# Row tables of the decays turned out of stage 0's table, and a prologue in a new order

## The chip, the cores and the metric

The kernel runs on one core of a Trainium2 chip. The metric is the device time of one launch, in microseconds. The five engines named below are TensorE (PE, with its weight loads as PEld), VectorE (DVE), ScalarE (ACT), GpSimd (POOL) and SyncE (SP, which only issues DMAs here). Each engine runs its own list of instructions in order, and waits on semaphores where it needs another engine or a DMA.

## The reference: what is computed

A linear attention with a decaying state (4 batches, 8 heads, 768 tokens, head size 48) is followed by a two-layer network. For each batch and head, over tokens t:

```
y[t]  = r[t] @ (state + outer(u * k[t], v[t]))
state = w[:, None] * state + outer(k[t], v[t])
x     = y with heads joined: (3072 tokens, 384)
h     = x @ w_in;  out = max(0.01 * h, h) @ w_out      # 384 -> 2048 -> 384
```

## The kernel before

The 768 tokens of a batch are cut into 6 chunks of 128. A **stage** n is one chunk of one batch, 24 in all: stages 0 to 3 are the first chunks of the four batches, 4 to 7 the second ones, and so on. Inside a chunk the recurrence is done by matrix products: r is scaled by w to the power (t - 64), k by w to the power (63 - t), so that the product of the two holds the decay between two tokens. The scale factors stand in **row tables** `qtab` and `ktab` (128 tokens x 384 head columns), which every stage except stage 0's first use multiplies into its r and k.

The work of one stage, with the names that the order list uses:

- `k3 r3 v3`: loads of 128 x 384 blocks in f32, cast to bf16 by the DMA (line 224, issued by POOL; stage 0's k and r come uncast over ACT's and SP's queues, line 215). `wi0` to `wi3` and `wo0` to `wo3` are quarters of the two weight matrices (lines 234 and 238, also POOL).
- `P3q`, `P3k`: DVE multiplies r by `qtab` and k by `ktab` (line 373).
- `T3q`, `t3q`: PE turns the product (four matmuls with the identity, line 436), ACT copies it out of PSUM (line 454; `t5q@` means that DVE does it). From stage 6 on a DMA transpose does both (`X6T`, line 378, issued by SP).
- `A3`: the 128 x 128 products of the turned pairs (PE, line 465). `M3a`, `M3b`: DVE masks them (lines 474 and 478).
- `X3 D3 Q3` (stages below 4) or `q4 Q4` (stages 4 and up): the diagonal term with u. `q4` is three DVE operations (lines 402, 404, 406) into `s_tok`; `Q4` is two POOL operations of 128 x 512 (line 413).
- `K3`, `S3`: the chunk's share of the state (PE, line 506) and its decay (DVE, lines 569, 572, 574).
- `Y3`, `y3`: the stage's output (PE, lines 597 and 604), copied by ACT into `xT` (line 618).
- `G3.1`, `g3.1`: a quarter of the first layer for one stage (12 matmuls, line 643; ACT, line 653). `J2.6`, `j2.6`: an eighth of it for the pair of stages 4 and 5 (6 matmuls of 256 columns, line 666; ACT, line 676).
- `H1`, `h1`: the second layer for one stage (16 matmuls, line 690; ACT, line 702; SP sends it out, line 704). It needs all of `w_out_sb`.
- `F6`: six matmuls on ones (line 271), whose result nobody reads. They wait only for the PSUM bank that comes next.

Two things set the order of the work. The **prologue**, up to stages 6 and 7, is the list `ORDER`, written out by hand: each name adds its instructions to its engine's list, so the list's order is the order on each engine, POOL's and SP's queues included. PSUM's eight banks are handed out in the same order, each from the bank that was given back longest ago. After it a loop over pairs of stages runs (lines 747 to 786): first layer of one pair, second layer of the pair before, attention of the pair after.

The tables before the change: `w` is loaded once as rows of one partition (line 709) and once by head (line 712). The by-head copy is turned by `Cw` (line 525), `Wl` takes its logarithm (line 544), and `E` makes `turned` (line 337): for each pair of heads the powers of w, with head columns on partitions and tokens along the row, q's half and k's half. `turned` scales stage 0's r and k after they were turned, so stage 0 doesn't wait for the row tables (`t0q`, `t0k`, line 449). The row copy goes another way: `bc` spreads it over 128 partitions by one-partition f32 matmuls (line 318), `lnw` takes its logarithm (line 325), and two exponentials with a scale for each token make `qtab` and `ktab` (line 332; `exps` makes the second scale, line 289).

Of the kernel before, what the change touches and what calls it, by code (L numbers as in the profile page):

```python
# [27 lines left out]
w8 k0 r0 w u8 u one trow ones tcol wlz r1 table tri id8 zr v0y k1 F6 Cw Wl exps id wi1 E v0z c0k@ k3 qk0 F11 T0k bc r3  # L28
c0q@ W wu8 t0k u16 T0q v0 lnw Cu t0q U qtab r2 C utab F2 A0 X0 P1q ktab v1 D0 M0a T1q wi3 P1k t1q P0k F6 T1k k2 P3k M0b
t1k F5 T3k v3 P3q F1 A1 t3k X1 Q0 r4 F1 D1 M1b T3q K0 k4 Y0 P2q t3q M1a K1 y0 A3 r5 Q1 T2q S1 G0.1 t2q k5 M3a Y1 g0.1  # L30
X3 wi2 G0.3 M3b y1 wi0 P2k G1.3 g0.3 S0 v2 D3 T2k g1.3 Q3 G1.1 t2k P4q v5 K3 P4k Y3 g1.1 X2 wo1 T4q P5q y3 D2 S3 T4k
t4q T5q v4 q5 G3.1 t4k A2 r6 t5q A4 g3.1 G3.3 wo3 P5k G1.2 M2a g3.3 Q5 M2b G3.2 g1.2 q4 G0.2 g3.2 G0.0 g0.2 k6 K2 g0.0
T5k Q2 G1.0 Q4 S2 t5k Y2 g1.0 A5 y2 G3.0 M5b k7 G2.3 M5a g3.0 M4a G2.2 wo2 g2.3 M4b K4 Y5 wo0 g2.2 S4 Y4 y5 r7 G2.1 P6q
y4 k8 J2.1 g2.1 J2.6 r8 q6 j2.1 J2.5 j2.6 r9 J2.3 j2.5 k9 P7k J2.4 j2.3 P6k J2.7 X6T Q6 j2.4 J2.2 j2.7 G2.0 j2.2 J2.0
g2.0 k10 H1 P7q j2.0 v11 q7 X7T v6 v7 P8k H0 h1 P8q Q7 q8 X8T P9q v8 H3 h0 v10 P9k q9 X9T r11 r10 A6 h3 A7 M6a H2 v9
M7a k11 M7b M6b Q9 K6 Y6 h2 S6 Y7 y6 K7 y7 Q8 K5 S7 S5
# [7 lines left out]
class Sched:  # L44
# [7 lines left out]

    def add(self, eng, emit, R=(), W=(), dma=None):
        o = Op()
        o.eng, o.emit, o.dma, o.inc, o.val = eng, emit, dma, False, None
        deps = []
        for key in R:
            w = self.writer.get(key)
            if w is not None:
                deps.append((w, True))  # L60
        for key in W:
            w = self.writer.get(key)
            if w is not None:
                deps.append((w, False))
            for r in self.readers.get(key, ()):
                deps.append((r, False))
        o.deps = []
        for d, raw in deps:
            if d.dma is None and d.eng == eng and dma is None and (eng == "pe" or not raw):
                continue  # L70
            if d is not o and d not in o.deps:
                o.deps.append(d)
        for key in R:
            self.readers.setdefault(key, []).append(o)
        for key in W:
# [51 lines left out]
def bass_rwkv5_eagle__then__act_leaky_relu_kernel(  # L127
# [13 lines left out]
    def SB(name, shape, dt=BF16):  # L141
        return ctx.enter_context(nc.sbuf_tensor(name, shape, dt))
# [7 lines left out]
    w_row = SB("w_row", [128, HD // 2], FP32)  # L150
    u_row = SB("u_row", [1, HD], FP32)
    one_row = SB("one_row", [128, 128], FP32)
# [7 lines left out]
    lnw = SB("lnw", [128, HD], FP32)  # L160
# [9 lines left out]
    kexp = SB("kexp", [128, 1], FP32)  # L170
# [137 lines left out]
    w_bank = []  # L308

    def spread_w():  # L310
        for half in range(2):
            w_bank.append(take())
        assert w_bank[1][1][1] == w_bank[0][1][1] + 1

        def emit():
            for half in range(2):
                at0 = slice(64 * half, 64 * half + 1)
                last = PE.matmul(w_bank[half][0][:, 0:192], one_row[at0, :], w_row[at0, :], start=True, stop=True)
            return last

        add("pe", emit, R=["one_row", "w_row"], W=[w_bank[0][1], w_bank[1][1]])

    def log_w():
        i = w_bank[0][1][1]
        add("act", lambda: A.activation(lnw[:, :].rearrange("p (two c) -> p two c", two=2),
                                        ps_all[:, i:i + 2, 0:192], AF.Ln),
            R=[w_bank[0][1], w_bank[1][1]], W=["lnw"])
        give(w_bank[0][1])
        give(w_bank[1][1])
# [366 lines left out]
    def g2_out(n, c0=0, c1=HD):  # L696
# [147 lines left out]
```

## Time and profile before

| what | before |
|---|---|
| time, median of 3 runs | 169.48 us (169.34 to 171.7) |
| the profiled execution's own time | 169.59 us |
| its span, first to last instruction | 167.8 us |
| PE busy | 162.7 us of the span |
| DVE, ACT, POOL busy | 110.5, 91.3, 110.8 us |
| fillings in the prologue (matmuls on ones) | 32 |
| first second-layer matmul in the chain | 38.02 us |

All times inside a profile are counted from the span's first instruction. A line of the timeline has the start in us, the time from there to the end of the last of the merged instructions, the engine, the line, the operation, and in brackets how long the engine had been idle and what ended that. Instructions of one engine overlap a little: the next one starts some 0.1 us before the one before has ended, so on a busy engine the distance between two starts counts. A line of the chain has start, length, and what the time is put down to. A second-layer block for one stage is 16 matmuls in 2.60 us, a `G` block 0.67 us, a `J` block 0.66 us.

### The profile page before, as it was taken

What the parts mean: (1) busy time and instruction counts of PE and PEld (TensorE: products, weight loads), DVE (VectorE), ACT (ScalarE), POOL (GpSimd) and SP (SyncE); (2) the same over time, 40 slices, a digit from 0 to 9 for tenths busy, and PEclk for the clock granted to TensorE, in tenths of its full rate; (3) what the DMA queues carried; (4) which work ended last, traced back from release to release, by engine and by line L of the source; (5) the groups of instructions that cost most, each with busy time, mean ns of one, the idle gap of its engine ahead of it and who ended that gap; (6) DMA issues with size and microseconds to landing.
All of it is one profiled execution on the core that took longest, in us unless ns stands there. A gap on an engine that the chain in (4) does not pass through costs nothing.

```text
span 167.8 us, 4861 instructions
## 1 busy us (share of the span) xinstructions
PE 162.7 (97%) x2089; PEld 123.1 (73%) x2089; DVE 110.5 (66%) x224; ACT 91.3 (54%) x168; POOL 110.8 (66%) x125
## 2 busy tenths in 40 slices
PE   5999999999999999999999999999999999999994
PEld 4577899996668768668668768678678678668563
DVE  7889696928885597596599998996996805000000
ACT  6944888893127437438437537537437447449221
POOL 8999969999997839939949976966960540000000
DMA  7999999999999995996994997995996111011012
GB/s 109 137 158 153 191 178 157 128 170 147 173 148 200 144 127 154 90 101 172 97 131 139 122 141 147 145 126 117 149 98 152 24 47 51 0 47 51 30 63 96
DMA packets 101267, 20.18 MB, mean 120 GB/s; under 512 B 94459, under 2 KB 101246, under 8 KB 101246
## 3 DMA queue, kind: packets, MB, share of 16 engines
q0 software_dynamic: 76512, 10.03, 95.5%
q1 hardware_dynamic: 23694, 9.65, 30.4%
q8 instruction: 16, 0.26, 0.6%
q10 hardware_dynamic: 1040, 0.20, 0.6%
q14 instruction: 5, 0.04, 0.1%
HBM read 20.45 MB, written 4.72 MB: 150 GB/s over the span
## 4 chain that ended last, share of the span: by engine, by line
PE 90%; POOL 4%; DMA 4%; ACT 1%; issue 0%; POOLq 0%
PE ps L690 38%; PE ps L666 32%; PE ps L643 7%; PE ps L604 6%; DMA v_sb<-in_v_dram 4%; PE ps L465 4%; PE ps L506 2%; POOL r_sb L224 2%; PE ps L436 1%; POOL k_sb L224 1%; ACT xT L618 1%; POOL v_sb L224 1%; POOL w_in_sb L234 0%; PE ps L597 0%; POOL trow L256 0%
## 5 line engine op out<-in xcount | busy, mean ns | idle before, releaser
L690 PE MATMUL ps<-w_out_sb,gT 128*128 128x384 bf16 (+2 forms) x400 | 65.6, 320 | 0.0
L413 POOL TENSOR_TENSOR at<-ident,s_tok 128x512 bf16<-128x512 bf16 x40 | 42.5, 1099 | 20.4 <-DVE s_tok L406 20.4
L666 PE MATMUL ps<-xT,w_in_sb 128*128 128x256 bf16 x480 | 55.1, 273 | 0.2 <-ACT xT L618 0.2
L690 PEld LDWEIGHTS ps<-w_out_sb,gT 128*128 128x128 bf16 x400 | 37.7, 98 | 22.4
L676 ACT ACTIVATE gT<-ps 128x512 bf16<-128x512 f32 x80 | 47.8, 597 | 9.2 <-PE ps L666 4.5
L666 PEld LDWEIGHTS ps<-xT,w_in_sb 128*128 128x128 bf16 x480 | 46.4, 98 | 6.9 <-ACT xT L618 0.3
L702 ACT ACTIVATE out_sb<-ps 128x384 f32<-128x384 f32 (+2 forms) x25 | 11.9, 478 | 55.6 <-PE ps L690 55.6
L478 DVE CAST_PREDICATED at<-mask,ps 128x512 bf16<-128x512 uint16 x40 | 24.8, 685 | 21.5 <-PE ps L465 21.5
L224 POOL DMA_DIRECT2D k_sb<-in_k_dram x23 | 21.5, 934 | 4.2 <-PE ps L666 4.2
L224 POOL DMA_DIRECT2D v_sb<-in_v_dram x24 | 22.0, 922 | 0.0
L224 POOL DMA_DIRECT2D r_sb<-in_r_dram x23 | 21.1, 923 | 0.1
L404 DVE TENSOR_TENSOR rku<-r_sb,ku 128x384 bf16<-128x384 bf16 x20 | 17.1, 856 | 0.7
L643 PE MATMUL ps<-xT,w_in_sb 128*128 128x128 bf16 x192 | 12.8, 224 | 0.0
L373 DVE TENSOR_TENSOR qk<-r_sb,qtab 128x384 bf16<-128x384 bf16 x23 | 10.2, 444 | 3.9 <-DMA r_sb<-in_r_dram 3.9
L574 DVE TENSOR_TENSOR st<-sum_t,wl 128x384 bf16<-128x384 bf16 x16 | 11.7, 730 | 0.5
L643 PEld LDWEIGHTS ps<-xT,w_in_sb 128*128 128x128 bf16 x192 | 11.5, 101 | 0.5
L406 DVE TENSOR_REDUCE s_tok<-rku 128x8 f32<-128x384 bf16 x20 | 11.1, 553 | 0.7
L618 ACT ACTIVATE xT<-ps 128x384 bf16<-128x384 f32 x24 | 10.8, 490 | 1.0 <-PE ps L604 0.8
L653 ACT ACTIVATE gT<-ps 128x512 bf16<-128x512 f32 x16 | 9.6, 599 | 2.7 <-PE ps L643 2.1
L604 PE MATMUL ps<-at,v_sb 128*32 128x128 bf16 x384 | 10.9, 223 | 0.0
L373 DVE TENSOR_TENSOR qk<-k_sb,ktab 128x384 bf16<-128x384 bf16 x23 | 8.8, 387 | 0.8 <-DMA k_sb<-in_k_dram 0.8
L604 PEld LDWEIGHTS ps<-tp,st 128*32 128x32 bf16 x240 | 7.2, 96 | 2.7 <-issue 2.5
(66 smaller groups left out, 122.5 us busy)
## 6 DMA issues: line engine op xcount, KB each, us to landing
out_dram<-out_sb SPq DMA_DIRECT2D x23, 192.0 KB, 2.2
v_sb<-in_v_dram POOLq DMA_DIRECT2D x24, 96.0 KB, 6.5
r_sb<-in_r_dram POOLq DMA_DIRECT2D x23, 96.0 KB, 5.9
k_sb<-in_k_dram POOLq DMA_DIRECT2D x23, 96.0 KB, 6.1
w_in_sb<-in_moe_w_in_dram POOLq DMA_DIRECT2D x4, 384.0 KB, 7.8
w_out_sb<-in_moe_w_out_dram POOLq DMA_DIRECT2D x4, 384.0 KB, 8.3
tp<-qk SPq DMA_TRANSPOSE x18, 5.1
k_f<-in_k_dram ACTq DMA_DIRECT2D x1, 192.0 KB, 2.7
```

The costliest lines, as they stand in the source:

```text
L224: add("pool", lambda: G.dma_start(dst, src), R=pace, W=[(which, n)], dma=f"{which}{n}")
L373: add("dve", lambda: V.tensor_tensor(qk[iq][:, H * half:H * half + H, 0:D], hd(src), hd(tab[:, :]), ALU.mult), R=[(name, n), "qk"[half] + ...
L404: add("dve", lambda: V.tensor_tensor(rku[i2][:, :], r_of(n), ku[i2][:, :], ALU.mult), R=[("r", n), ("ku", i2)], W=[("rku", i2)])
L413: add("pool", lambda hh=hh, s_of=s_of: G.tensor_tensor(at[ia][:, hh, :, :], ident[:, :].unsqueeze(1).to_broadcast([128, NP, 128]), s_of.un ...
L478: add("dve", lambda: V.copy_predicated(at[n % NAT][:, hh, :, :], mask[:, :].bitcast(mybir.dt.uint16).unsqueeze(1).to_broadcast([128, NP, 1 ...
L604: last = PE.matmul(ps_y[32 * q:32 * q + 32, 128 * s:128 * s + 128], a, m, start=not whole and step == 0, stop=step == len(columns[q]) - 1)
L618: add("act", lambda: A.activation(xT[m % NX][:, :, 128 * half:128 * half + 128], ps_y[:, 0:HD].rearrange("p (s t) -> p s t", t=128), AF.Copy),
L643: last = PE.matmul(ps_g[:, 128 * f:128 * f + 128], w_in_sb[:, s, 128 * fb:128 * fb + 128], xT[ix][:, s, t], start=s == 0, stop=s == NSL - 1)
L666: last = PE.matmul(ps_g[:, 256 * f:256 * f + 256], w_in_sb[:, s, 128 * fb:128 * fb + 128], xT[ix][:, s, :], start=s == 0, stop=s == NSL - 1)
L676: add("act", lambda: A.activation(gT[ig][:, 2 * j:2 * j + 2, :].rearrange("p f t -> p (f t)"), ps_g[:, :], AF.Prelu, alpha=0.01), R=[key], ...
L690: last = PE.matmul(ps_o[:, 0:c1 - c0], gT[ig][:, s, 128 * half:128 * half + 128], w_out_sb[:, s, c0:c1], start=s == 0, stop=s == NFB - 1)
L702: add("act", lambda: A.activation(out_sb[io][:, c0:c1], ps_o[:, 0:c1 - c0], AF.Copy), R=[key], W=held)
```

## The change

The row tables are now taken from `turned`. After `E`, `TQ` turns the four q tiles of `turned` on PE with the identity into one PSUM bank, `TK` the four k tiles into another; `qtab` and `ktab` are each one ACT copy out of PSUM that skips the unused columns. The row load of w, `one`, `bc`, `lnw`, `exps` and the two exponentials are gone, with their tiles. The rest of the change is the list `ORDER`, which is new from end to end. Stage 0's casts `c0k` and `c0q` move from DVE to ACT, `t5q` from ACT to DVE. The fillings are 58 in place of 32 (`F18`, `F4`, `F10`, `F1`, `F3`, `F16`, `F3`).

```
-    def spread_w():            # bc: PE, w_row spread by one_row
-    def log_w():               # lnw: ACT
-    def table(dst, exps, name, read):
-        add("act", lambda: A.activation(dst[:, :], lnw[:, :], AF.Exp, scale=exps[:, 0:1]),
-            R=["lnw", read], W=[name + "tab"])
...
+    def turn_table(half):
+        ps_t, key = table_bank[half] = take()
+
+        def emit():
+            for p in range(NP):
+                last = PE.matmul(ps_t[:, 128 * p:128 * p + 128], turned[:, NP * half + p, :], ident[:, :],
+                                 start=True, stop=True)
+            return last
+
+        add("pe", emit, R=["ident"] + [("turned", p) for p in range(NP)], W=[key])
+
+    def table(half, eng):
+        ps_t, key = table_bank[half]
+        dst = hd((qtab, ktab)[half][:, :])
+        src = ps_t[:, :].rearrange("p (h e) -> p h e", e=E)[:, :, 0:D]
...
+            add("act", lambda: A.activation(dst, src, AF.Copy), R=[key], W=["qk"[half] + "tab"])
+        give(key)
```

The lists that follow for each engine, up to the point where the prediction reads them:

```
PE before:   F6 Cw F11 T0k bc T0q Cu U F2 A0 D0 T1q F6 T1k F5 T3k F1 A1 F1 D1 T3q K0 Y0 K1 A3 T2q G0.1 Y1 G0.3 G1.3 D3
             T2k G1.1 K3 Y3 T4q D2 T4k T5q G3.1 A2 A4 G3.3 G1.2 G3.2 G0.2 G0.0 K2 T5k G1.0 Y2 A5 G3.0 G2.3 G2.2 K4 Y5 Y4
             G2.1 J2.1 J2.6 J2.5 J2.3 J2.4 J2.7 J2.2 G2.0 J2.0 H1 H0 H3 A6 A7 H2 K6 Y6 Y7 K7 K5
PE after:    F18 Cw F4 T0k F10 T0q F1 TQ TK Cu F3 A0 T2q D0 T2k F16 A2 Y0 D2 T1k F3 T1q K2 G0.1 Y2 A1 K1 D1 T3k T5q T3q
             U G2.1 A3 G0.3 D3 K3 Y1 G2.3 G1.3 Y3 T4k G1.1 G3.2 G3.1 T5k T4q G3.3 G0.0 A4 A5 G3.0 K0 G1.2 K5 G2.2 G2.0
             G1.0 K4 Y5 Y4 G0.2 J2.7 J2.5 J2.6 J2.4 J2.0 J2.1 J2.2 H2 H3 H1 A6 A7 H0 K7 Y6 Y7 K6 J2.3
DVE after:   v0z ones v0y tri id wlz id8 zr qk0 wu8 t0k t0q P2q X0 C P2k M0a Q0 M0b X2 P1k M2a P1q M2b Q2 S2 P3k X1 P5q
             P3q M1a t5q@ Q1 X3 M1b M3b M3a Q3 P4k q5 S3 P4q P5k S1 q4 P0k M5a M5b S0 M4a P7k P6k M4b S4 S5 q6 P6q P7q ...
ACT after:   k0 table c0k Wl E c0q qtab ktab W t2q t2k y0 t1k u16 t1q g0.1 y2 t3k t3q utab g2.1 g0.3 y1 ...
POOL before: trow tcol r1 k1 wi1 k3 r3 v0 r2 v1 wi3 k2 v3 r4 k4 r5 k5 wi2 wi0 v2 v5 wo1 v4 r6 wo3 Q5 k6 Q4 k7 wo2 wo0 r7 ...
POOL after:  v0 tcol trow r2 k2 wi1 r5 k1 r1 v2 k3 v1 r3 wi3 v3 k5 k4 wi2 r4 wi0 wo0 v5 k6 k7 v4 wo1 Q5 r6 Q4 wo3 wo2 r7 ...
```

More of the change, by code (lines that the diff above doesn't have):

```diff
@@ L27 @@
 ORDER = """
[L28 to L36, printed above, removed]
+w8 k0 r0 u8 u v0z v0 ones table v0y tcol trow r2 tri id wlz id8 k2 zr F18 Cw c0k Wl wi1 F4 T0k qk0 E r5 c0q F10 T0q wu8
+k1 F1 TQ t0k r1 TK t0q qtab Cu ktab P2q v2 F3 A0 X0 W C P2k T2q k3 M0a D0 T2k t2q Q0 v1 t2k M0b F16 A2 r3 X2 Y0 P1k M2a
+wi3 D2 y0 T1k P1q M2b v3 t1k F3 T1q K2 u16 Q2 G0.1 k5 S2 t1q Y2 g0.1 P3k k4 X1 A1 y2 P5q K1 P3q D1 T3k wi2 M1a T5q t3k
+T3q U t5q@ r4 t3q G2.1 Q1 utab A3 wi0 X3 g2.1 G0.3 M1b wo0 M3b D3 K3 g0.3 Y1 v5 M3a G2.3 y1 Q3 k6 G1.3 P4k g2.3 q5 k7
+Y3 g1.3 T4k y3 v4 G1.1 t4k S3 G3.2 wo1 g1.1 P4q P5k G3.1 Q5 g3.2 S1 T5k g3.1 T4q G3.3 q4 t4q G0.0 t5k r6 g3.3 A4 A5
+g0.0 P0k G3.0 Q4 M5a K0 G1.2 g3.0 M5b S0 K5 G2.2 g1.2 wo3 G2.0 M4a g2.2 wo2 P7k G1.0 g2.0 P6k M4b r7 K4 Y5 g1.0 S4 Y4
+r9 y5 G0.2 S5 y4 k9 J2.7 g0.2 q6 r8 J2.5 j2.7 J2.6 k8 j2.5 J2.4 P6q j2.6 Q6 J2.0 X6T j2.4 J2.1 j2.0 J2.2 j2.1 k10 H2
+j2.2 P7q q7 v6 X7T v7 P9q v8 H3 P9k h2 q9 X9T Q7 P8q H1 h3 Q9 q8 v9 P8k A6 h1 X8T A7 M6b H0 Q8 M6a M7b M7a v11 K7 Y6 h0
+r10 S7 Y7 y6 K6 k11 y7 J2.3 S6 v10 j2.3 r11
 """
@@ L149, in bass_rwkv5_eagle__then__act_leaky_relu_kernel @@
     v_sb = SB("v_sb", [128, NST, H * E])
-    w_row = SB("w_row", [128, HD // 2], FP32)
     u_row = SB("u_row", [1, HD], FP32)
-    one_row = SB("one_row", [128, 128], FP32)
     u_row16 = SB("u_row16", [1, HD])
@@ L708, in bass_rwkv5_eagle__then__act_leaky_relu_kernel @@
     single = {
-        "w": lambda: add("sp", lambda: SP.dma_start(
-            w_row[0:65:64, :], dram(w, 0, [[HD // 2, 2], [1, HD // 2]])),
-            W=["w_row"], dma="w"),
         "w8": lambda: add("sp", lambda: SP.dma_start(w_head[:, :, 0:D], twice(w)), W=["w_head"], dma="w8"),
```

32 lines of the change are left out of this document (9 added, 23 removed).

## The prediction

> **What bounds the kernel now.** I read the engine totals first, then the chain of work that ended last, then the timeline around the places that the chain names.
>
> ```profile
> PE 162.7 (97%) x2089; PEld 123.1 (73%) x2089; DVE 110.5 (66%) x224; ACT 91.3 (54%) x168; POOL 110.8 (66%) x125
> ...
> DMA  7999999999999995996994997995996111011012
> ```
>
> PE is busy all through, and the DMA engines are full from about 4 us to 63 us. Either can set the prologue's pace; the chain says which does where:
>
> ```profile
> 7.58 6.63 DMA v_sb<-in_v_dram
> ...
> 14.26 0.50 PE ps L506 x4
> ...
> 38.02 7.80 PE ps L690 x48
> 45.82 0.55 PE ps L465 x16
> ...
> 49.80 0.89 ACT xT L618 x2
> ...
> 50.74 5.41 PE ps L666 x48
> ```
>
> Up to 14.26 the chain is POOL's issues and one transfer (v1). From there it is PE without a break, but for 0.3 us at 50.4 where PE waits for `xT`. The loop after 50.74 is the same in both kernels and PE-bound, so the change is worth what it moves the loop's start. Three marks carry the sum: the first second-layer block (38.02), stage 7's `A7` (46.03, the second half of the 45.82 piece) and 50.74.
>
> Two further limits stand close behind PE, in the timeline:
>
> ```profile
> 38.32 0.36 DVE L373 TENSOR_TENSOR qk<-r_sb,qtab 128x384 bf16<-128x384 bf16 x1 [3.85 <-DMA r_sb<-in_r_dram]
> ...
> 22.63 2.09 POOL L413 TENSOR_TENSOR at<-ident,s_tok 128x512 bf16<-128x512 bf16 x2 [1.61 <-DVE s_tok L406]
> ...
> 23.93 1.01 DVE L402 TENSOR_TENSOR ku<-k_sb,u_tab 128x384 bf16<-128x384 bf16 x1
> ```
>
> The first is `P7q`, held by r7's landing at 38.3; its DMA transpose, issued at 38.7, lands 6.8 us later by its own row, at 45.5, and `A7` runs at 46.03: 0.5 us of slack. The other two show a DVE product of two SBUF operands (0.35 us elsewhere) held until POOL's two products of `Q5` are over.
>
> PE's matmul spacing halves inside the prologue, while the granted clock reads 1.000 throughout:
>
> ```profile
> 4.88 1.01 PE L318 MATMUL ps<-w_row,one_row 1*128 1x192 f32 x4
> ...
> 9.74 0.74 PE L271 MATMUL ps<-ones 128*128 128x128 bf16 x5
> ...
> 15.64 1.33 PE L643 MATMUL ps<-xT,w_in_sb 128*128 128x128 bf16 x12
> ...
> 19.14 0.83 PE L643 MATMUL ps<-xT,w_in_sb 128*128 128x128 bf16 x12
> ```
>
> One matmul takes 0.31 us to its end when slow, 0.22 when fast, so the spacings are (0.74-0.31)/4 = 107 ns, and (0.83-0.22)/11 = 55 ns; in the third line some nine are slow, and the turn lies near 16.6.
>
> **The tables.** POOL issues v0 (1.05 us) before the iotas, so these end at 2.4 instead of 1.35; DVE has the two memsets of `v_sb` (0.27 + 1.12) ahead of the masks. `id8` and the gap in `w_head` are ready at 3.35, `Cw` runs at 3.4 instead of 2.43. `E` ended 1.91 us after `Wl` began; with `c0k` ahead of it on ACT (k_f lands at 3.45, a cast near 0.5) `Wl` begins at 3.95 and `turned` is done at 5.85, against 4.76. `c0q` follows on ACT to 6.25, so `T0q` runs at 6.3 against 5.83. `TQ` and `TK` are eight matmuls at 107 ns, 0.86 us, against 0.94 of `bc`; the copies, by the row of the 128x384 copy (L355, 0.49 us), replace 0.49 + 0.61 + 0.60 on ACT. No copy with this gap pattern is shown; the 128x384 and 128x512 copies bound it at 0.49 and 0.60, I take 0.49. `qtab` is ready at 8.0 (before 7.08), `ktab` at 8.45 (before 8.15), `A0` runs at 8.3 (before 7.37). All this is 0.3 to 1.1 us later, and it is hidden: the first readers, P2q and P2k, feed `A2` behind `F16`, and what follows waits for k1. Without that cover it would cost up to 0.9.
>
> **Loads.** From wi1 (9.7) to wo0 (36.5) 17 slices and 7 weight blocks landed in 26.8 us; a block took 1.95 (wi3 after v1), so a slice 0.77 on average. The new list has the same bytes up to wo2 as the old up to wo0 and starts 0.6 earlier, but the second issue falls at 2.4 as before. I take wi1 at 10.1 (four items, not three), then k1 11.6, r1 12.4, v2 13.15, v1 14.7, r3 15.45, wi3 17.4, v3 18.2, k4 19.7, wi2 21.65, r4 22.4, wi0 24.4, v5 27.1, v4 29.4, wo2 36.0. Every one is 0.3 to 1 us before its reader below.
>
> **The new order on DVE and PE**, by distances between starts in the old timeline (`P` 0.27, `M` 0.60, `Q` 0.48, `X` 0.33, `q` 1.25, `S` 0.5; PE: `G` 0.67, `T` 0.22, `A` 0.27, `K` 0.18, `Y` 0.4 to 0.45). `P1k` starts with k1 at 11.85, then M2a 12.2, P1q, M2b, Q2 13.7, S2 at 14.6 (it waits for `K2`), X1 15.4, M1a 16.25, `t5q@` (0.57 and 0.69 bound it, from the casts and masks; I take 0.6), Q1, X3 17.9, M1b, M3b, M3a, Q3 20.0, P4k 20.5, q5 20.8 to 22.05. DVE has 0.5 us of waits in these 10 us: it is the bound here. PE follows it: G0.1 14.4, G2.1 17.05 (its bank comes from M1a), G0.3 18.0, Y1 19.0, Y3 20.7, G1.1 21.35, G3.2 22.0, G3.1 to 23.35.
>
> **Here comes a new stall.** `Q5` starts when q5 is done, since POOL's issues end at 21.8, and runs 22.1 to 24.2. P4q and P5k are due at 22.6 and are products of two SBUF operands, so by the row of 23.93 they wait until 24.2. `T5k`, next on PE, runs at 24.85 instead of 23.35: 1.4 us of idle PE (the second M of the old order, fed from PSUM, ran through `Q5` unhurt). After it PE has no wait: from T5k on 8 `G` (5.36), 7 `J` (4.62), T5k, T4q (0.46), A4, A5 (0.54), K0, K5, K4 (0.54), Y5, Y4 (0.9) make 12.4 us, and the first second-layer block (`H2`) is at 37.25, 0.8 earlier than 38.02; wo2 at 36.0 is in time.
>
> How long the hold lasts is the open size. A later row (40.11, a DVE product of 2.52 us over both of POOL's products at 40.32 to 42.40) says that DVE doesn't get in between the two; I take both. The Trainium skill, "SBUF — State Buffer", section "Who interferes with whom", says that a DVE instruction with two SBUF inputs and a GpSimd instruction that reads SBUF exclude each other for the whole of one instruction; that is rival 2 below.
>
> Then `A7`: r7 is issued at 30.1 (before 30.41) and lands near 37.3 (one slice after wo2, between 0.8 and the 1.8 us of the old trace), P7q ends at 37.65, the transpose is issued at 38.0 and lands 6.8 later, at 44.8. `A7` is due at 37.25 + 7.8 + 0.27 = 45.3, so it doesn't wait, and is 0.7 early. Behind it the new order has J2.3 (0.66) more and K5 (0.17) less, and the 0.3 at `xT` goes, since K6 and J2.3 (0.83) cover the 0.75 from Y7's issue to y7. SP's queue changes too: X8T now stands behind the output DMA of h1, goes out at 45.8 and lands by the longest early row of a transpose (8.8) at 54.6; `A8` is due at 55.3, so this costs nothing until it is 0.7 later. Sum: -0.7 + 0.5 - 0.3 = -0.5. Against the profiled 169.59 that is 169.1, against the median, 0.11 lower, 169.0. **I forecast 169.0**, its own range 168.7 to 169.5.
>
> **The clock.** I price the stretch from G0.1 with the fast spacing. The new list keeps PE without a gap over 0.2 us from 8.0 to 14.4; before, the turn came 2.3 us after the last gap of that size, and a stretch from 8.3 to 10.3 hadn't been enough. So it should come between 10.3 and 14.4. The Trainium skill, "TensorE: Matmul & The Clock Gate", Part 1, says that activity is judged in free-running windows of 3.4 us, and one busy window releases the clock: by it the turn falls between 11.4 and 14.8, the same for the sum.
>
> **Rivals.**
> 1. *POOL does not hold P4q.* PE then reaches H2 at 35.8 and the loads are the bound: wo2 at 36.0 keeps H2 there, and X7T keeps `A7` to 44.8. That is -1.2 + 0.2, 168.5. For: the order of starts hangs on q5 to 0.5 us. Against: P4q stands half a microsecond behind it on DVE. 0.15.
> 2. *The hold lasts one of POOL's two products.* P4q goes at 23.15, P5k behind it at 23.4 or after the second; with the first, T5k runs at 23.8, H2 at 36.2, and `A7` at 44.8 again: 168.5. Against: the row of 40.11. 0.1. The sentence of the Trainium skill quoted above would have it so.
> 3. *Slower: r7 comes late.* POOL's wo3, wo2 and r7 stand behind `Q4`, which waits for q4 on DVE, and that for r4, k4 and for what `Q5` held up. I have q4 at 26.5. The place is `A7` behind X7T; r7's landing at 38.3 makes a loss of nothing gained, and from there it costs 1 us for each us. With q4 at 27.7, r7 is issued at 31.3, lands (7.9 us, its old row) at 39.2, the transpose at 46.7: 170.3. With the longest landing of this stretch (9.8 us) and q4 on time it is 39.9 and 171.0. For: 0.5 us of slack before, and DMA engines that are full. Against: r7 has the same number in the queue of loads. 0.2.
> 4. *The change doesn't do what its fillings say:* spacing slow to 16.6. G0.1, Y2, A1, K1 and the turns then take 0.9 more, and DVE's M1a waits for it: 169.9. 0.08.
>
> The forecast has 0.45; 0.02 is left for anything else. The **range** goes from rivals 1 and 2 with the loads 1 us earlier (the first issue's 0.6 and a short step from wo2 to r7; 167.5) to rival 3's upper end (171.0). No case passes 166.1, the landing of wo2 and r7 forbids it: faster by over 2% (about what a measurement of this kernel can tell from no change) 0.04; slower than 172.9 would need r7 after 41.5: 0.07; within, 0.89.
>
> **What would show it.** `qtab`'s copy near 7.5; matmul spacing 55 ns before 14.5; in the waits a T5k behind P4q/P5k of over 1 us, at 23 to 25, with a 1.5 us or longer L373 on DVE under POOL's L413; H2 at 37.2; no `xT` wait ahead of the first L666 of the loop. It would be wrong if k1 landed after 12.5 (everything on DVE moves with it), if PE stood still before H2 for `w_out_sb`, or if `A6`, `A7` waited for their transposes.

## The result, and the profile after

The changed kernel takes **170.46 us** (median of 20 runs, 169.66 to 171.17), the kernel before 169.56 us in the 20 runs beside them. The ratio is **1.0051, interval 1.0034 to 1.0068**: a small loss, where a gain of 0.5 us was forecast. The profiled execution took 170.09 us with a span of 168.3, against 169.59 and 167.8. So the two profiles show 0.5 us of the 0.9 us between the medians. In the table of runs below, the ratios and the medians of e1 and e8 leave out executions that took over 1.5% longer than the fastest of the same kernel (three of e1's twelve, one of e8's).

One correction first: the section on the change says 58 fillings. The seven entries listed there add up to 55, and the profile agrees: 2116 matmuls, 27 more than before, are 23 more fillings, and four more matmuls for the tables (eight in place of the four of `bc`).

Line numbers behind the first functions are lower by 12 in the changed kernel: L373 is now L361 (products with the row tables), L402 and L404 are L390 and L392, L413 is L401 (`Q`), L478 is L466 (second half of the masks), L604 is L592 (`Y`), L666 is L654 (`J`).

The engine totals and the row of DMA activity, from the profile page of the changed kernel:

```profile
PE 161.6 (96%) x2116; PEld 122.6 (73%) x2116; DVE 110.2 (66%) x221; ACT 91.0 (54%) x168; POOL 111.1 (66%) x125
...
DMA  7999999999999996995994995994999111011012
```

PE is busy for 1.1 us less although it has more matmuls, and the DMA engines are as full as before. The totals don't tell what is late. The chain of work that ended last does; its columns are start, length, and what the time is put down to. Changed kernel:

```profile
15.61 7.52 DMA r_sb<-in_r_dram
...
23.15 1.80 DVE qk L361 x2
...
26.75 2.28 POOL at L401 x2
...
32.27 8.17 DMA k_sb<-in_k_dram
...
40.46 2.30 DVE qk L361
...
44.28 1.13 DVE ku L390
...
45.43 1.09 DVE rku L392
...
47.36 2.40 DVE at L466 x4
49.77 0.14 issue
49.90 0.57 PE ps L592 x28
```

Before, PE carried the chain from 14.26 on without a break but one. Now it hands over to DVE, POOL and the loads, and PE has the chain again only from 49.90. From 40.46 to 49.77 the chain is DVE. DVE's timeline shows what it had to do (changed kernel; columns as in the section on the profile before):

```profile
23.15 1.53 DVE L361 TENSOR_TENSOR qk<-r_sb,qtab 128x384 bf16<-128x384 bf16 x1 [0.90 <-DMA r_sb<-in_r_dram]
...
40.46 2.30 DVE L361 TENSOR_TENSOR qk<-k_sb,ktab 128x384 bf16<-128x384 bf16 x1 [0.48 <-DMA k_sb<-in_k_dram]
...
44.19 1.20 DVE L390 TENSOR_TENSOR ku<-k_sb,u_tab 128x384 bf16<-128x384 bf16 x1
45.43 1.08 DVE L392 TENSOR_TENSOR rku<-r_sb,ku 128x384 bf16<-128x384 bf16 x1
46.55 0.55 DVE L394 TENSOR_REDUCE s_tok<-rku 128x8 f32<-128x384 bf16 x1
47.01 0.35 DVE L361 TENSOR_TENSOR qk<-k_sb,ktab 128x384 bf16<-128x384 bf16 x1
47.28 2.48 DVE L466 CAST_PREDICATED at<-mask,ps 128x512 bf16<-128x512 uint16 x4
```

And POOL's timeline at the same places, changed kernel:

```profile
22.32 2.13 POOL L401 TENSOR_TENSOR at<-ident,s_tok 128x512 bf16<-128x512 bf16 x2
...
40.46 2.08 POOL L401 TENSOR_TENSOR at<-ident,s_tok 128x512 bf16<-128x512 bf16 x2
...
44.09 2.21 POOL L401 TENSOR_TENSOR at<-ident,s_tok 128x512 bf16<-128x512 bf16 x2 [1.55 <-DVE s_tok L394]
```

The reader is to lay the two over each other. Every DVE product of two SBUF operands that is 0.35 us elsewhere and 1.1 to 2.3 us here runs beside a POOL product: `P4q` beside `Q5`, `P9k` beside `Q7`, and the two products of `q8` beside `Q9`. The new list places `q8` and `P8k` ahead of the masks of stages 6 and 7, so these wait for all of it. They start at 47.28; before, they started at 46.26, held by PE's `A6` and `A7`. DVE's timeline of the kernel before:

```profile
46.26 2.48 DVE L478 CAST_PREDICATED at<-mask,ps 128x512 bf16<-128x512 uint16 x4 [0.60 <-PE ps L465]
```

Behind the masks stand `Y6` and `Y7`.

PE's timeline of the changed kernel shows the tables, a stall for the weights wi2 that hadn't been forecast, the forecast stall of `T5k`, and the new wait ahead of `Y7`:

```profile
7.24 0.81 PE L307 MATMUL ps<-ident,turned 128*128 128x128 bf16 x8
...
22.99 1.51 PE L631 MATMUL ps<-xT,w_in_sb 128*128 128x128 bf16 x24 [0.51 <-DMA w_in_sb<-in_moe_w_in_dram]
25.00 0.62 PE L424 MATMUL ps<-ident,qk 128*128 128x128 bf16 x8 [0.50 <-DVE qk L361]
...
49.90 0.24 PE L592 MATMUL ps<-tp,st 128*32 128x128 bf16 x4 [0.23 <-DVE at L466]
```

Where the 0.5 us came from follows from five starts on PE that both kernels have:

| start on PE | before | after | change of the distance |
|---|---|---|---|
| first second-layer block | 37.85 | 37.57 | |
| `A7` | 45.98 | 45.89 | -0.09 in all up to here |
| `Y6` | 49.18 | 49.10 | +0.01 |
| the first `K` behind `Y7` (`K7` before, `K6` after) | 50.08 | 50.41 | **+0.41** |
| `A8` | 56.09 | 56.58 | +0.16 |

The sum is 0.49; PE's last matmul ends at 165.94 instead of 165.44. The loop itself is not longer. So this execution lost 0.41 us between `Y6` and `Y7`, where the masks came late, 0.16 behind them, where the longer end of the list (`J2.3`) is, and gained 0.09 in everything ahead.

### The profile page after: what moved, and what is told of

Read it like the earlier page. It is cut to its first block, busy times and chain, and to the rows that moved or that the text cites. A ratio compares the mean times of both kernels' runs of the same rounds, so it can differ in the third digit from the quotient of the medians.

```text
span 168.3 us, 4915 instructions
## 1 busy us (share of the span) xinstructions
PE 161.6 (96%) x2116; PEld 122.6 (73%) x2116; DVE 110.2 (66%) x221; ACT 91.0 (54%) x168; POOL 111.1 (66%) x125
## 4 chain that ended last, share of the span: by engine, by line
PE 69%; POOL 12%; DMA 9%; DVE 7%; issue 1%; ACT 0%; POOLq 0%; DVEq 0%
PE ps L678 31%; PE ps L654 29%; DMA k_sb<-in_k_dram 5%; PE ps L592 5%; DMA r_sb<-in_r_dram 4%; POOL r_sb L220 3%; DVE qk L361 3%; PE ps L453 3%; POOL k_sb L220 3%; POOL v_sb L220 2%; PE ps L494 2%; DVE at L466 1%; POOL at L401 1%; POOL w_in_sb L230 1%; DVE rku L392 1%; DVE ku L390 1%
## 5 line engine op out<-in xcount | busy, mean ns | idle before, releaser
L401 POOL TENSOR_TENSOR at<-ident,s_tok 128x512 bf16<-128x512 bf16 x40 | 42.8, 1101 | 21.0 <-DVE s_tok L394 21.0
L654 PE MATMUL ps<-xT,w_in_sb 128*128 128x256 bf16 x480 | 54.9, 273 | 0.0
L678 PEld LDWEIGHTS ps<-w_out_sb,gT 128*128 128x128 bf16 x400 | 37.7, 98 | 22.4
L654 PEld LDWEIGHTS ps<-xT,w_in_sb 128*128 128x128 bf16 x480 | 46.4, 98 | 6.7
L466 DVE CAST_PREDICATED at<-mask,ps 128x512 bf16<-128x512 uint16 x40 | 25.0, 684 | 21.8 <-PE ps L453 21.8
L392 DVE TENSOR_TENSOR rku<-r_sb,ku 128x384 bf16<-128x384 bf16 x20 | 17.8, 892 | 0.7
L606 ACT ACTIVATE xT<-ps 128x384 bf16<-128x384 f32 x24 | 10.9, 491 | 2.3 <-PE ps L592 2.2
L361 DVE TENSOR_TENSOR qk<-r_sb,qtab 128x384 bf16<-128x384 bf16 x23 | 9.1, 400 | 4.5 <-DMA r_sb<-in_r_dram 4.1
L631 PEld LDWEIGHTS ps<-xT,w_in_sb 128*128 128x128 bf16 x192 | 10.9, 98 | 1.3 <-DMA w_in_sb<-in_moe_w_in_dram 0.7
L562 DVE TENSOR_TENSOR st<-sum_t,wl 128x384 bf16<-128x384 bf16 x16 | 10.7, 672 | 0.5
L592 PE MATMUL ps<-at,v_sb 128*32 128x128 bf16 x384 | 10.7, 219 | 0.0
L361 DVE TENSOR_TENSOR qk<-k_sb,ktab 128x384 bf16<-128x384 bf16 x23 | 9.9, 434 | 0.7 <-DMA k_sb<-in_k_dram 0.7
L592 PEld LDWEIGHTS ps<-tp,st 128*32 128x32 bf16 x240 | 7.2, 96 | 3.1 <-issue 2.5
```

The costliest lines, as they stand in the source:

```text
L361: add("dve", lambda: V.tensor_tensor(qk[iq][:, H * half:H * half + H, 0:D], hd(src), hd(tab[:, :]), ALU.mult), R=[(name, n), "qk"[half] + ...
L392: add("dve", lambda: V.tensor_tensor(rku[i2][:, :], r_of(n), ku[i2][:, :], ALU.mult), R=[("r", n), ("ku", i2)], W=[("rku", i2)])
L401: add("pool", lambda hh=hh, s_of=s_of: G.tensor_tensor(at[ia][:, hh, :, :], ident[:, :].unsqueeze(1).to_broadcast([128, NP, 128]), s_of.un ...
L466: add("dve", lambda: V.copy_predicated(at[n % NAT][:, hh, :, :], mask[:, :].bitcast(mybir.dt.uint16).unsqueeze(1).to_broadcast([128, NP, 1 ...
L592: last = PE.matmul(ps_y[32 * q:32 * q + 32, 128 * s:128 * s + 128], a, m, start=not whole and step == 0, stop=step == len(columns[q]) - 1)
L631: last = PE.matmul(ps_g[:, 128 * f:128 * f + 128], w_in_sb[:, s, 128 * fb:128 * fb + 128], xT[ix][:, s, t], start=s == 0, stop=s == NSL - 1)
```

## The experiments

All names of stages and operations are those of the list. A table of the marks of all runs comes first; the ratios are against the kernel before on the same chip, and "A6 to A7" is the distance of two starts on PE that is 0.23 when `A7` waits for nothing.

| kernel | ratio, interval | median, us | first H | A6 to A7 | `A7` | last PE end |
|---|---|---|---|---|---|---|
| before | | 169.56 | 37.85 | 0.23 | 45.98 | 165.44 |
| after | 1.0051 (1.0034, 1.0068) | 170.46 | 37.57 | 0.42 | 45.89 | 165.94 |
| e1_tables_alone | 1.0021 (0.9997, 1.0046) | 169.57 | 37.42 | 0.24 | 45.55 | 165.00 |
| e2_order_alone | 1.0073 (1.0054, 1.0092) | 170.34 | 37.68 | 0.91 | 46.49 | 166.12 |
| e3_masks_before_q8 | 1.0031 (1.0013, 1.0049) | 169.96 | 37.39 | 0.48 | 45.77 | 165.48 |
| e4_fills_as_few | 1.0062 (1.0037, 1.0086) | 170.32 | 38.12 | 0.49 | 46.51 | 166.13 |
| e5_tables_two_more_on_act | 1.0003 (0.9977, 1.0029) | 169.18 | 37.38 | 0.23 | 45.51 | 164.97 |
| e6_p5k_before_q5 | 1.0022 (0.9994, 1.0050) | 169.63 | 36.95 | 0.45 | 45.30 | 164.93 |
| e7_r7_one_later | 1.0077 (1.0056, 1.0099) | 170.61 | 37.41 | 1.28 | 46.59 | 166.22 |
| e8_tables_k6_behind | 0.9996 (0.9975, 1.0016) | 169.26 | 36.59 | 0.59 | 45.08 | 164.38 |
| e9_stage1_over_sp | 1.0221 (1.0187, 1.0255) | 172.72 | 40.53 | 0.23 | 48.66 | 167.95 |
| e10_stage1_over_sp_fills | 1.0204 (1.0163, 1.0244) | 172.75 | 40.35 | 0.23 | 48.48 | 167.77 |
| e11_iotas_first | 1.0019 (0.9997, 1.0041) | 169.66 | 36.98 | 0.31 | 45.19 | 165.49 |
| e12_stage1_over_sp_u_first | 1.0046 (1.0013, 1.0079) | 169.95 | 38.09 | 0.23 | 46.22 | 166.54 |

How far a mark of one profile can be trusted is seen in e5 and e8. Their lists are the same up to `Q9`, and yet the first second-layer block is at 37.38 in one and 36.59 in the other. So a difference of a few tenths in the first H between two profiles is no evidence by itself; distances between neighbouring instructions, and waits, are.

### The tables alone, and the order alone

e1_tables_alone has the old list with the new tables:

```
- w8 k0 r0 w u8 u trow one ones tcol ... exps ... F11 T0k bc ... lnw qtab ...
+ w8 k0 r0 u8 u trow ones tcol ...          ... F11 T0k TQ TK ...    qtab ...
```

> The old order list with only the tables changed: TQ and TK stand where bc stood, the row load of w, one, exps and lnw are gone. Theory A (the loss comes from the new order of DVE's queue at the prologue's end, and the tables are hidden): the time of the kernel before, within 0.2 us (ratio 0.999 to 1.001), qtab ready 0.3 to 0.6 us sooner than before and nothing late behind it. Rival B (turning the tables on TensorE costs time by itself): 0.5 to 0.9 us slower, ratio 1.003 to 1.005.

e2_order_alone has the new list with the old tables:

```
- w8 k0 r0 u8 u v0z v0 ones ... r2 tri ... c0q F10 T0q ... F1 TQ t0k r1 TK t0q qtab ...
+ w8 k0 r0 w u8 u v0z v0 one ones ... r2 exps tri ... c0q bc F10 T0q ... F1 t0k r1 t0q lnw qtab ...
```

> The new order list with the old tables: bc behind T0k, lnw ahead of qtab, one and exps on VectorE, w's row load third on SyncE's queue. Theory A: the time of the changed kernel (ratio to before 1.003 to 1.007), since the loss is in the order. Rival B: the time of the kernel before or better (0.997 to 1.000), since the costly part is gone.

Measured: 1.0021 and 1.0073. The intervals don't meet, so **the loss is in the order, not in the tables**. In e2 the profile has the wait of rival 3: PE stands 0.52 us ahead of `A7` for the transposed r of stage 7. In e1 the body of the kernel is 0.44 us shorter (last matmul at 165.00), and its time isn't; the next run is about that. A few tenths in the body of a single profile are no evidence by themselves, as e5 and e8 show.

### A long tail in one profile

In e1 the time from the last matmul to the end of the span is 3.26 us, in all other runs here 2.33 to 2.42. The last 64 KB of the output landed late. The view of DMA issues between 164.5 us and the end, with size and the time from issue to landing, for e1:

```profile
q14 instruction: 1, 0.01, 0.9%
...
out_dram<-out_sb SPq DMA_DIRECT2D x1, 128.0 KB, 1.7
out_dram<-out_sb SPq DMA_DIRECT2D x1, 64.0 KB, 2.5
```

A transfer of instructions (the `instruction` queue, 0.01 MB) lay at 166.4 to 167.0, between the packets of that last output. e5_tables_two_more_on_act shifts where in ACT's list of instructions the end lies, by two copies of one column that nobody reads:

```
- X0 P1q ktab v1 D0 ...
+ X0 P1q ktab padA padB v1 D0 ...
+        "padA": lambda: add("act", lambda: A.activation(spare[:, 0:1], tcol[:, :], AF.Copy), ...),
+        "padB": lambda: add("act", lambda: A.activation(spare[:, 1:2], tcol[:, :], AF.Copy), ...),
```

> The old order with the new tables (as in e1), and two activations of one column on ScalarE behind ktab, whose results nobody reads; they bring ScalarE's instruction count in the profile from 192 back to 194. In e1's profile TensorE's last matmul ended 0.44 us sooner than in the kernel before (165.00 against 165.44), yet the last output DMA landed 2.5 us after its issue instead of 1.5, and a transfer of 8 KB of instructions ran between, at 166.4 to 167.0 (before: 165.7 to 166.1). Theory E (code loading by an engine at the very end sits between the last output's packets, and where it falls hangs on that engine's instruction count): the instruction transfer is back near 165.3 to 165.8, the last output lands 1.5 us after its issue, and the time is 168.5 to 169.2, ratio 0.994 to 0.999. Rival (the long landing in e1 was a single event, or comes with the new tables themselves): the ratio stays at 1.001 to 1.003.

Measured: the same view of e5:

```profile
q14 instruction: 1, 0.01, 0.5%
...
out_dram<-out_sb SPq DMA_DIRECT2D x1, 128.0 KB, 1.8
out_dram<-out_sb SPq DMA_DIRECT2D x1, 64.0 KB, 1.5
```

The transfer of instructions now lies at 165.1, the output lands in 1.5 us, and the tail is 2.35 again, with two instructions more. The median goes from 169.57 to 169.18, and the intervals of the two ratios overlap. The ratio of 1.0003 meets neither the 0.994 to 0.999 that the theory had nor the rival's 1.001 to 1.003. In every other profile here the transfer of instructions lies 0.1 to 0.2 us ahead of the last output's issue (in e5, 165.13 and 165.31), and that output lands in 1.5 to 1.6 us; e1 alone has it 1.0 us behind the issue. So a transfer in that place and a late output went together once. That it delayed the output, and that the two instructions moved it, is not shown: a single event remains possible.

In e5 the tables alone give 1.0003: **no difference that these runs can tell from none.** The 0.4 us that the body shows against the kernel before is within what e5 and e8 differ by.

### The masks ahead of q8

e3_masks_before_q8 changes the place of two names of the new list:

```
- Q9 q8 v9 P8k A6 h1 X8T A7 M6b H0 Q8 M6a M7b M7a v11
+ Q9 v9 P8k A6 h1 X8T A7 M6b H0 M6a M7b M7a q8 Q8 v11
```

> The changed kernel with one move: q8 (three VectorE operations) goes from ahead of P8k to behind the masks of stages 6 and 7. Theory A: VectorE reaches the masks when A6 ends (near 45.8 instead of 47.28), Y6 no longer waits, and the 0.42 us that TensorE stood still at 49.1 to 49.6 go: 0.3 to 0.45 us faster than the changed kernel, ratio to before 1.002 to 1.004 where the changed kernel has 1.005. Rival B (the loss is already made ahead of the first second-layer block) or the view that the masks are only named and PE waits for another thing: no change against the changed kernel.

Measured: DVE's timeline of e3 at that place:

```profile
44.00 1.20 DVE L361 TENSOR_TENSOR qk<-k_sb,ktab 128x384 bf16<-128x384 bf16 x1
45.80 2.48 DVE L466 CAST_PREDICATED at<-mask,ps 128x512 bf16<-128x512 uint16 x4 [0.59 <-PE ps L453]
48.19 0.35 DVE L390 TENSOR_TENSOR ku<-k_sb,u_tab 128x384 bf16<-128x384 bf16 x1
```

The masks wait for PE again, as before the change, not PE for the masks. `q8` runs behind them, beside no POOL product, at 0.35 us. `Y6` and `Y7` follow each other without a gap, and the last matmul ends at 165.48, 0.46 us sooner and 0.04 behind the kernel before. So the 0.41 us of the profile is the masks behind `q8`, shown by taking it away.

Not every execution pays it. e2 and e4 have the masks behind `q8` too, and in their profiles `K` follows `Y6` by 0.90 us, as in the kernel before. In e2 the masks start even later than in the changed kernel:

```profile
47.38 2.47 DVE L478 CAST_PREDICATED at<-mask,ps 128x512 bf16<-128x512 uint16 x4
```

But `A7` ran at 46.49 there instead of 45.89, and when `Y7`'s turn came (50.10) the masks were done. The two waits hide each other: the late masks keep `Y7` until 49.9 even if `A7` is on time, and a late `A7` alone brings it to 50.1. The first `K` behind `Y7` is at 50.41, 50.60 and 50.61 in the changed kernel, e2 and e4, against 50.08 before. In the times, 1.0051 becomes 1.0031 with the masks ahead; the intervals overlap, so a gain in time isn't shown, and 1.0031 is still a loss.

### What is left: r7, P7q, X7T, A7

e7_r7_one_later is e3 with two loads in POOL's queue exchanged, r7 and r9:

```
- M4b r7 K4 Y5 g1.0 S4 Y4 r9 y5
+ M4b r9 K4 Y5 g1.0 S4 Y4 r7 y5
```

> e3 with r7 and r9 swapped in GpSimd's list of loads, so that r7 lands one slice (0.75 us) later. Theory A (A7 stands behind r7, P7q and its DMA transpose, and nothing is left between): A7 0.6 to 0.8 later than in e3 (46.4 to 46.6), the loop's start and the time 0.5 to 0.8 us later, ratio to before 1.006 to 1.008. Rival: there is slack, A7 and the time stay, ratio 1.002 to 1.004.

Measured: PE's timeline of e7:

```profile
45.31 0.40 PE L453 MATMUL ps<-tp 48*128 48x128 bf16 x8
46.59 0.40 PE L453 MATMUL ps<-tp 48*128 48x128 bf16 x8 [0.89 <-DMA tp<-qk]
```

r7 landed at 38.33 instead of 37.78, `A7` ran 0.82 us later than in e3, and the loop began 0.82 later; the time went from 1.0031 to 1.0077. So **`A7` stands behind r7 and its transpose with no slack** in the new order, and what they lose goes into the time. r7's landing is not all of it: in e4 r7 landed at 37.28, 0.8 us sooner than in the changed kernel, but its transpose took 8.7 us from issue to landing (46.37), and `A7` ran at 46.51. The column "A6 to A7" says the same of the other runs: it is 0.31 to 0.91 in the kernels with the new list whose loads of stage 7 weren't touched, and 0.23 or 0.24 with the old list, but for e8, where the first H was the earliest of all. In the profiled execution of the changed kernel that wait is 0.19 us; in e2 it is 0.68. This would account for the 0.4 us of the medians that the two profiles don't show, since other executions of the changed kernel can fall as e2's did; that is an argument from the other kernels' profiles, not shown for this kernel itself.

### The stall at Q5

e6_p5k_before_q5 is e3 with `P5k` ahead of `q5`, so that POOL's `Q5` can't hold it, `T4q` behind `G0.0`, and `A5` ahead of `A4`:

```
- P4k g2.3 q5 k7 Y3 ... P4q P5k G3.1 Q5 g3.2 S1 T5k g3.1 T4q G3.3 q4 t4q G0.0 t5k r6 g3.3 A4 A5
+ P4k P5k g2.3 q5 k7 Y3 ... P4q G3.1 Q5 g3.2 S1 T5k g3.1 G3.3 q4 t5k G0.0 r6 g3.3 T4q g0.0 t4q G3.0 A5 A4
```

> e3 (masks ahead of q8) and P5k moved ahead of q5 on VectorE, T4q behind G0.0 on TensorE, A5 ahead of A4: T5k no longer waits behind P4q, which waits for r4 and then for Q5's two products on GpSimd. The stall of 0.5 us at 24.8 that the prediction named goes. Theory A (the loads cap what can be gained: wo2 for the first second-layer block, r7 and its transpose for A7): first second-layer block at most 0.3 earlier, A7 where e3 has it (45.77), time within 0.15 us of e3, ratio to before 1.002 to 1.004. Rival F (as the prediction had it, the stall is on the path that sets the end): 0.4 to 0.5 us faster than e3, ratio 0.999 to 1.001.

Measured, in DVE's timeline of e6:

```profile
22.49 2.16 DVE L361 TENSOR_TENSOR qk<-r_sb,qtab 128x384 bf16<-128x384 bf16 x1
```

`P4q` is still held through both products of `Q5`, but nobody waits for it: e3's idle time of 0.47 us ahead of `T5k` (24.82) is gone. In its place PE stands 0.39 us inside `T5k`, ahead of its last matmul, for which the profile names no cause. The first H comes 0.44 sooner than in e3 and the last matmul 0.55 sooner, but PE was 0.47 ahead at `T4k` already (21.47 against 21.94), before the stall. From `T4k` to the first H both kernels take 15.5 us, so no gain of the move itself can be seen, and what the stall is worth stays open. In time, 1.0022 against 1.0031 with wide intervals is inconclusive. `A7` still waits 0.2 us behind `A6`.

### Fewer fillings

e4_fills_as_few is the changed kernel with 19 fillings instead of 55 (`F18` to `F6`, `F16` to `F6`, `F4` and `F10` out; the expectation counts three too many in both).

> The changed kernel with 22 fillings in place of 58 (F6 F1 F3 F6 F3 F3). In the changed kernel the matmul spacing halves at 7.6 us, before at 16.6. Theory C (the denser fillings turn the clock early, and this is worth something): the spacing turns after 10 us, G0.1 and what follows is late by up to 0.9 us, and the time rises by 0.1 to 0.6 us over the changed kernel. Theory A alone, with the loads capping A7 (X7T behind r7): the early clock is worth nothing, the time stays within 0.2 us.

Measured, in PE's timeline of e4 (columns as before):

```profile
10.39 0.74 PE L267 MATMUL ps<-ones 128*128 128x128 bf16 x6
11.29 0.40 PE L453 MATMUL ps<-tp 48*128 48x128 bf16 x8 [0.16 <-ACT tp L442]
```

The six fillings at 10.39 stand some (0.74 - 0.31)/5 = 86 ns apart on average, between the slow 107 and the fast 55, and the eight matmuls behind them are all fast; so the turn to the fast spacing lies among the six, near 10.9, against 7.7 in the changed kernel. The time is 1.0062 against 1.0051, with intervals that overlap. e2, with the fillings of the changed kernel, turned only at 13.9, and its first H is 0.1 us behind (37.68 and 37.57). **3.2 us of earlier full speed are worth at most some tenths of a per cent here**, since PE waits for loads and for DVE in that stretch.

### The start of the tables

e11_iotas_first is e3 with the iotas ahead of the first load on POOL:

```
- w8 k0 r0 u8 u v0z v0 ones table v0y tcol trow r2
+ w8 k0 r0 u8 u v0z tcol trow v0 ones table v0y r2
```

> e3 with GpSimd's iotas ahead of v0's load, as in the kernel before, instead of behind it. The prediction had the later masks, Cw, turned and tables (0.3 to 1.1 us) hidden. If so: turned 0.7 to 1.1 earlier, the loop's start and the time as in e3 within 0.2 us, ratio 1.002 to 1.004. If they are not hidden: 0.4 us or more faster than e3, ratio 1.001 or less.

Measured: `turned` was done about 0.3 us sooner than in e3 (0.7 to 1.1 were expected), and `qtab`'s copy began at 7.12 instead of 7.90. The loop's first block began at 49.47 against 50.06, 0.59 us sooner, where the expectation allowed 0.2. The gain was lost inside the loop, where PE waited for the transpose of stage 11; PE's timeline of e11:

```profile
68.79 0.40 PE L453 MATMUL ps<-tp 48*128 48x128 bf16 x8 [0.49 <-DMA tp<-qk]
```

The last matmul ended at 165.49, against 165.48 in e3, and the ratio is 1.0019 against 1.0031, with intervals that overlap. The 0.59 us are within what e5 and e8 differ by, so e11 doesn't settle whether the late tables cost something. In the changed kernel itself DVE stands idle for 0.21 us ahead of `P1k` until k1 has landed (12.09), behind the first readers of the tables; that speaks for hidden tables.

### Attempts at a faster kernel

e8_tables_k6_behind is e5 with `K6` and `S6` behind `Y7`:

```
- Q9 K6 Y6 h2 S6 Y7 y6 K7 y7 Q8 K5 S7 S5
+ Q9 Y6 h2 Y7 y6 y7 K6 S6 K7 Q8 K5 S7 S5
```

> e5 and one move: K6 goes from ahead of Y6 to behind Y7, so that three short matmul groups (0.5 us), not two, stand between Y7 and the loop's first block, which waits for Y7's copy. Theory: the 0.35 us gap ahead of the loop's first block shrinks by K6's 0.17 us, and the time is 0.1 to 0.2 us under e5. Rival: Y6, now earlier, waits for the masks of stage 6, and nothing is gained.

Measured: the distance from `A7` to `Y6` falls from 3.19 to 3.04. That from `Y7` to the loop's first block stays at 1.16, now with the third group in it and no wait of PE's. So the 0.15 us are in the profile, as expected; the ratio is 0.9996 against 1.0003, no gain that these times can tell.

e9_stage1_over_sp is e8 with stage 1's k and r loaded uncast over SP's queue, so that POOL's queue has two loads less at the start; e10_stage1_over_sp_fills adds seven fillings to it; e12_stage1_over_sp_u_first has the small loads of u ahead of the two:

```
- TURNED, DIAG, CARRY, EXACT, RAW, VISIT, LATE = 6, 4, 4, 1, 1, 3, 3
+ TURNED, DIAG, CARRY, EXACT, RAW, VISIT, LATE = 6, 4, 4, 2, 1, 3, 3
- w8 k0 r0 u8 u trow ones tcol wlz r1 table ... v0y k1 F6
+ w8 k0 r0 r1 k1 u8 u trow ones tcol wlz table ... v0y F6      (e9; e10 with F10 and F14 for F6 and F11)
+ w8 k0 r0 u8 u r1 k1 trow ones tcol wlz table ... v0y F6      (e12)
```

> e8 with stage 1's k and r loaded uncast over SyncE's queue like stage 0's r, and taken out of GpSimd's list; stage 1's two products then read f32 (0.55 us each, not 0.35). In every profile so far A7 began 7.7 to 8.6 us after r7 landed, and r7 stands behind 19 slices and 8 weight blocks in GpSimd's queue of loads. Theory A (the loads cap the prologue): the list is two slices (1.75 us of issue, 1.5 of landing) shorter, v0, v1, wi1 and r7 land 0.7 to 1.5 earlier, A7 no longer waits, TensorE's own work is the bound, and the time is 0.3 to 1.0 us under e8, ratio 0.994 to 0.998. Rival: the two transfers take the same room on the DMA engines, or hold up stage 0's, and the ratio stays at 0.999 to 1.001.

> e9 with the first two fillings longer (F6 and F11 become F10 and F14), in gaps that TensorE has there in any case. Theory C (an early clock is worth something once the loads don't cap): matmul spacing halves sooner than in e9, and 0.1 to 0.5 us less time than e9. Rival: no difference beyond 0.1 us, as between the changed kernel and e4.

> e9 with u8 and u ahead of r1 and k1 on SyncE's queue. In e9 u_head landed 7.2 us after its issue, at 10.6, behind the two transfers of stage 1 in the same queue, and wu_head, u_row and with them stage 0 stood still for 5 us. Theory A (as stated for e9): with that gone, v0, v1 and r7 land earlier than in e8 and the time is 0.3 to 1.0 us under e8, ratio 0.994 to 0.998. Rival: stage 1's k and r land no sooner than over GpSimd's queue and take room from its loads, ratio 1.000 or more.

Measured: e9 lost 2.2%. The view of waits of e9 (time in all, how often, the longest) has the cause:

```profile
DVE wu_head L331 <- DMA u_head<-in_u_dram: 5.2, 1, 5.2
```

The small load of u stood behind the two large ones in SP's queue and landed 7.2 us after its issue; stage 0 waited for it. More fillings changed nothing (e10): the fast spacing came no sooner, at 16.4 against 16.2, and the ratio is 1.0204. With u ahead (e12) that wait is gone, and the chain of e12 begins with the moved load:

```profile
2.90 7.55 DMA k_f<-in_k_dram
```

k1 landed at 10.45; over POOL's queue, in the kernel before, DVE's product with it ran at 8.79 already. v0, v1 and r7, which were to land earlier, landed 0.4, 0.4 and 2.3 us later than in e8. So the move brings nothing, and e12's ratio is 1.0046. In its profiled execution PE also stood 0.86 us ahead of `Y7`, which started at 50.68 behind v7's landing at 50.54. No version here is faster than the kernel before by an interval that leaves out 1.

## Why the prediction was wrong, point by point

**What bounds the kernel: right.** The loop is the same, and what counts is where it starts. The range, and that the difference is within 2%, held.

**The tables: right in their times.** Predicted and measured: `Cw` 3.4 and 3.86, `TQ` 6.8 (from `T0q` at 6.3) and 7.24, `qtab`'s copy 7.5 to 8.0 and 7.86 to 8.35 (0.49 us, as taken from the nearest copy), `ktab` ready 8.45 and 8.73, `A0` 8.3 and 8.44. That all of it is hidden agrees with the idle time ahead of `P1k` and with e5; e11 doesn't settle it.

**The loads: right but for the end.** wi1 10.1 and 10.50, k1 11.6 and 12.09, v1 14.7 and 14.87, wi3 17.4 and 17.45, v5 27.1 and 27.59 are a few tenths late, which is where the sum of 0.77 us for a slice and 1.95 for a weight block leads. wi2 was 1.3 late (21.65 and 22.94), and this is the 0.51 us of idle PE at 22.99. r4 was 0.7 late (22.4 and 23.12), and `P4q` began with it. wo2 came at 37.27 instead of 36.0, which is still 0.3 ahead of the block that reads it, and r7 at 38.09 instead of 37.3.

**The stall at `Q5`: right in its place, its mechanism and its hold, too large on PE.** `q5` ended at 21.78 (22.05 forecast), `Q5` ran 22.32 to 24.45 (22.1 to 24.2), and `P4q` ended behind both of POOL's products. `T5k` waited 0.50 us, not 1.4, because PE came to `G3.2` 1.0 us later than forecast (22.99 and 22.0), most of it through wi2. The two waits together are 1.0. One reading under it is weaker than it looks: the product in the row of 23.93 began 0.25 us into POOL's second product, so it shows the hold of one; the hold over both rests on the row of 40.11 alone.

Rival 2 lets the hold last one of POOL's two products. That fell for `P4q` and `P9k` here and for e6's `P4q`, which began between 0 and 0.83 us into the first product and ended with the second. It stands for `q8` (1.20 and 1.08 us, one POOL product each), and at `Q5` itself in other kernels: in e3 `P4q` took 0.87 us, to the end of the first product, and `P5k` 1.19, to the end of the second; e2, e7 and e11 are like it. `T5k` was free only behind the second in either case. The Trainium skill, "SBUF — State Buffer", section "Who interferes with whom", says that a DVE instruction with two SBUF inputs contends with a GpSimd instruction that reads SBUF, and calls the lock exclusive. The held products agree with that; it doesn't say who gets in between two POOL instructions that follow each other, and that stays open.

**First second-layer block: 37.25 forecast, 37.57 measured.** The gain was 0.28, not 0.8; 0.17 of the difference is that the forecast counted from 38.02, the chain's mark, where PE started at 37.85.

**`A7`: the step that first failed.** "`A7` is due at 37.25 + 7.8 + 0.27 = 45.3, so it doesn't wait, and is 0.7 early." It ran at 45.89. 0.3 of the missing 0.6 is the later first block, 0.2 is the wait behind r7, and the rest is the three blocks, which take 7.9 us by their starts, not 7.8. r7 landed 0.8 later than taken and its transpose took 7.3 us, not 6.8 (7.4 to 8.7 in e3, e7, e2 and e4), so that it landed at 45.8 instead of 44.8. The place is rival 3's, `A7` behind X7T. Its reason isn't: q4, which the rival has late, was done at 26.65 (26.5 in the forecast), and r7 was issued 0.4 later than forecast, at 30.5. The rival's own price of 0.8 to 1.5 us was too high for this execution, and its statement that 38.3 gives "a loss of nothing gained" is what the marks show. e7 shows that it decides from there on.

**Behind `A7`: the step that was missing.** The sum carried what `A7` gains to the loop with no cost in between but the list on PE. DVE's list behind `A7` was priced for the stretch up to 24 us only. `q8` and `P8k` ahead of the masks, and the hold by `Q7` and `Q9` on them, were not counted, although it is the mechanism that was priced at `Q5`. That is the 0.41 us of this profile, and e3 shows it. With the masks done at 49.8, `Y7` could not have come before 49.9 even if `A7` had run at 45.3 as forecast, so this step alone would have undone the forecast gain.

**The end of the list: right.** J2.3 more, K5 less and the wait for `xT` gone were to cost 0.2 us; measured 0.16.

So the sum of -0.7 + 0.5 - 0.3 = -0.5 became -0.09 + 0.01 + 0.41 + 0.16 = +0.49 in the profiled executions.

**The clock.** The turn to the fast spacing came at 7.7, ahead of the forecast 10.3 to 14.4, so rival 4 fell. The forecast's lower end rested on a misread stretch: in the kernel before PE had no gap over 0.25 us from 4.34 to 10.48, not only from 8.3 to 10.3, and the spacing stayed slow. It hardly matters: e4 turned at 10.9. The Trainium skill, "TensorE: Matmul & The Clock Gate", Part 1, says that the window runs free, so that the same kernel can turn at different moments. The range of 11.4 to 14.8 that was worked out from it is not what was measured in the changed kernel; e2, with the same fillings, turned at 13.9. e1 and e5, alike on PE up to there, turned at 15.8 and 11.4, which agrees with a turn that isn't fixed by the list alone.

## What to carry to other kernels

Price the whole of the list that a change reorders on every engine that feeds the bound, up to the point where both kernels are alike again: a hold that was found and priced at one place (a DVE product beside POOL's products) was the cause of the loss at a later place that wasn't read. A gain ahead of a load that stands at its limit isn't a gain: work out when the last load of the stretch lands plus all that follows from it (here DVE product, transpose, product), and let that set the mark. Two late inputs of neighbouring instructions hide each other: taking one away gains only what the other leaves. Before a difference between two single profiles is taken for the effect of an edit, look at two kernels that are alike up to the mark, and at the time from the last matmul to the end.

## What the runs showed of the hardware that was not expected

- A DVE product of two SBUF operands that meets two POOL products, one right behind the other, lasts until both are over (1.53 us at `Q5`, 2.30 at `Q7`, 2.16 in e6), or only as long as one (1.20 and 1.08 us at `Q9`, 0.87 and 1.19 at `Q5` in e3). Which of the two happens isn't explained by its start: 1.20 started 0.10 us into a POOL product, 2.30 at the same moment as one, 2.16 started 0.23 us into one, and 0.87 started 0.39 us into one. In e3 a product that began 0.66 us ahead of POOL's two (39.60) lasted until both were over, 2.97 us. In the kernel before one took 1.20 us (33.26) with no POOL product beside it, while POOL issued loads; why is open.
- In one profile (e1) a transfer of 8 KB of instructions lay 1.0 us behind the issue of the last output, and that landed 2.5 us after its issue instead of 1.5. In all others the transfer lay ahead of that issue, and there was no delay.
- The granted clock is a poor sign of the early slow spacing. In the kernel before it reads 1.000 while matmuls are 107 ns apart. In e9, where PE stood 4.66 us idle, it reads 0.50 from 10 to 15 us, with the same spacing: five fillings in 0.74 us are (0.74 - 0.31)/4 = 107 ns.
- In e9 and e12 the uncast loads of stage 1 over SP's queue took 5.7 to 8.4 us to land at the start of the kernel, and in e9 a small load behind them in the queue took 7.2.
